# Filter table filled by ScalarE from one PSUM bank and by VectorE from the other, with a new instruction order

## The chip, the cores and the metric

The kernel runs on one core of a Trainium2 chip. It uses five engines: TensorE (PE, matrix products into PSUM), VectorE (DVE), ScalarE (ACT), GpSimd (POOL) and SyncE (SP), which issues the DMAs. The metric is the device time of one execution in microseconds (us), lower being better. Times are medians over several executions; a profile comes from one execution and has a time of its own.

## The reference

Four sequences of 768 steps with 8 heads of width 48 go through a gated linear recurrence; its output, 384 channels wide, goes through a block that multiplies a circular convolution over time (by Fourier transform) with two gates.

```
for t in range(S):                       # S = 768, per batch and head
    cur = outer(u * k[t], v[t])
    y[t] = r[t] @ (state + cur)
    state = w[t][:, None] * state + outer(k[t], v[t])
x = y.transpose(0, 2, 1, 3).reshape(B, S, 384)

proj = x @ w_proj                        # three parts: x1, x2, x3
H = rfft(filter_fft, n=S, axis=0)
x2c = irfft(rfft(x2, n=S, axis=1) * H, n=S, axis=1)
out = (x1 * x2c * x3) @ w_out
```

Inputs and output are float32.

## The kernel before

Each of the 4 sequences is cut into 6 chunks of 128 steps, 24 chunks numbered through. A chunk goes through the function `first`: the running sum of log w by two matrix products (`cs`), its exponential in place in PSUM (`ex`, ScalarE), a product with k and r (`kq`, VectorE, L1344), eight transposes (`tr`), a copy (`qk`), the scores within the chunk (`sc`), their triangular mask (`mt` on VectorE or ScalarE, `mc` on GpSimd where ScalarE made the copy), the state (`ki`, `kv`, `su`), the output (`yi`, `ys`, `y`, `xn`) and its transpose (`yt`, `xT`). Chunks are loaded alone or in pairs by `group`, four loads a chunk (w, k, r, v: `lw`, `lk`, `lr`, `lv`), which also makes the diagonal term (`rk`, `ru`, `rh`, `cc`, `vc`: products of tensors in SBUF).

When a sequence's chunks are done, `second` runs the block: projections `p` and `q` with their gate products (`cp`, `cq`, `gq`), the middle part `xw`, sums and differences of its two halves (`sd`), the forward transform `f` (three blocks of frequencies; copied by `cf` to the tile X), the product with the filter table (`u0`, `u1` into U, their sum into P; that sum's steps are also called `p`, as p0.0 or p3.1, on VectorE, where the projections p0.0.0 are TensorE's), the inverse transform `E` with the sums of even and odd parts (`cE`, `aE`, `dE`), the gate (`yE`), the output projection `o` with its copy `co` and store `so`. The last sequence (3) does this in smaller pieces, so that its stages overlap.

The filter table is made once, by `spectrum`, in the middle of the first second half: `fsd0` and `fsd1` (VectorE) take sum and difference of the two halves of the loaded filter; `h0`, `h1`, `h2` (TensorE) transform them, each into two PSUM banks, one with the cosine part and one with the sine part; and the copies scale both parts into the tile hh, twice each, one sign changed. In the kernel before, `hc` (ScalarE) reads both banks for one half of hh and `hg` (VectorE) reads both banks for the other half. All later `u` read hh.

Nothing schedules this at run time. Every engine runs its instructions in the order in which they stand, and waits by semaphores. The order is a table (`ORDER`, about a thousand lines): each line names a step, the engine that does it (P, A, D, G, S; M and N one instruction over both score banks on VectorE or ScalarE, V an addition on VectorE, C a GpSimd cut over both, "-" not needed), the PSUM bank where it takes one, and sometimes another step after which a GpSimd instruction is made to start (a tie, given to the framework as a dependency with the reason "port"). Lines `warm n` are products of a zero tile without use, placed where TensorE has nothing else. Loads stand in the table too, in the order in which SP issues them.

Of the kernel before, what the change touches and what calls it, by code (L numbers as in the profile page):

```python
# [21 lines left out]
L = 128  # L22
# [15 lines left out]
ADD, DVE2, ACT2, POOL2, FOLD, FULL, BLOCK = "V", "M", "N", "C", "Q", "F", "B"  # L38
# [257 lines left out]
rk4 G
xT4 A
xw0.0 P 0
ex6 A
cq0.2.0 D  # L300
cxw0.0 A
gq0.2.0 -
cs7 P 6
kq6 D
xw0.2 P 2
ex7 A
ph6 A
kq7 D
cxw0.2 A
p0.2.1 P 0  # L310
cp0.2.1 A
ru4 D
xw0.4 P 4
tr6 P 2
tr7 P 0
ph7 A
p0.0.1 P 6
cxw0.4 A
vb4 A
sd0.0.0 D  # L320
sd0.1.0 D
kv6 P 4
qk7 A
su6 D
rh4 D
cc4 D
qk6 A
cp0.0.1 A
q0.2.1 P 5
sc7 P 3  # L330
sc6 P 1
mt6.0 M
mt7.1 -
mt6.1 -
mc7.1 -
mc6.0 -
vc4 G rh4
ki7 P 0
cq0.2.1 D
gq0.2.1 -  # L340
kv7 P
q0.0.1 P 6
cq0.0.1 D
su7 D
f0.2 P 1
mt7.0 N
ln5 A
mc7.0 C
fsd0 D
fsd1 D  # L350
lw14 S
yi6 P 3
in A
cf0.2 A
gq0.0.1 -
mc6.1 -
y6 P
lw15 S
xn6 A
yi7 P 5  # L360
ys7 P
y7 P
xn7 A
cs8 P 0
ex8 A
cs9 P 2
yt7 P 5
lr14 S
lk15 S
lr15 S  # L370
lk14 S
xT7 A
ex9 A
kq8 D
f0.1 P 6
cf0.1 A
lv13 S
lv12 S
kq9 D
h1 P 4  # L380
ph8 A
hg1 D
f0.0 P 6
hc1 A
ph9 A
cf0.0 A
ln6 A
rk5 G fsd1
ru5 D
rh5 G ru5  # L390
h2 P 2
lw17 S
vb5 G ru5
lv17 S
lw16 S
hc2 A
h0 P 4
hg2 D
hc0 A
hg0 D  # L400
yt6 P 2
tr8 P 6
u00.0 D
tr9 P 7
ki8 P 0
kv8 P
xT6 A
qk8 A
sc8 P 5
xw1.0 P 3  # L410
qk9 A
su8 D
lv15 S
mt8.0 N
u10.0 D
ki9 P 2
p0.0 D
sc9 P 0
kv9 P
cxw1.0 A  # L420
mt8.1 -
lk16 S
mc8.1 -
mt9.1 -
lv14 S
lr17 S
lr16 S
lk17 S
mt9.0 N
cs11 P 6  # L430
cs10 P 4
ex10 A
su9 D
kq10 D
ex11 A
warm 5 3
E0.2 P 0
gq0.0.0 -
cc5 D
cwout A  # L440
ph10 A
cE0.2 A
E0.0 P 2
kq11 D
aE0.2.0 D
E0.1 P 4
cE0.0 A
ph11 A
tr11 P 6
aE0.0.1 D  # L450
aE0.0.0 D
mc8.0 C p0.0
vb6 A
aE0.2.1 D
cE0.1 A
mc9.0 C p0.0
vc5 G
tr10 P 7
qk11 A
aE0.1.1 D  # L460
aE0.1.0 D
yi8 P 2
ys8 P
ki10 P 0
qk10 A
y8 P
xn8 A
kv10 P
sc11 P 6
su10 D  # L470
yt8 P 4
yi9 - 0
dE0.2.1 -
sc10 P 2
mt11.0 M
ln7 A
mt11.1 -
mt10.1 -
mc9.1 -
xT8 A  # L480
ys9 P
y9 P
xn9 V
mt10.0 N
cs12 P 4
# [3 lines left out]
rk6 G  # L489
ru6 G  # L490
rh6 D
cc6 D
p1.0.0 P 0
mc10.0 C rh6
vc6 G rh6
kq12 D
ph12 A
lv16 S
lw18 S
lw19 S  # L500
lr19 S
kq13 D
cp1.0.0 A
q1.0.0 P 2
ph13 A
lk19 S
lk18 S
lr18 S
yi11 - 6
yi10 - 0  # L510
tr12 P 4
yt9 P 5
cq1.0.0 D
qk12 A
mc11.1 -
dE0.1.1 -
mc11.0 -
dE0.2.0 -
dE0.1.0 -
dE0.0.0 -  # L520
mc10.1 -
xT9 A
ys10 P
ys11 P
y10 P
y11 P
rk7 G
xn11 V
tr13 P 4
xn10 V  # L530
rk8 G
qk13 A
p1.2.0 P 5
yt11 P 2
xw1.2 P 6
ln8 A
cp1.2.0 A
xT11 A
lw21 S
lv18 S  # L540
lv19 S
lk20 S
yt10 P 4
dE0.0.1 -
yE0.2 D
yE0.0 D
yE0.1 D
sc13 P 0
ru7 D
xT10 A  # L550
gq1.0.0 -
mt13.1 -
cxw1.2 A
cs15 P 2
mt13.0 M
ex15 A
xw1.4 P 4
cs14 P 6
kq15 D
cxw1.4 A  # L560
ex14 A
o0.2 P 0
ph15 A
kq14 D
sd1.1.0 D
rh7 D
p1.0.1 P 4
q1.0.1 P 2
co0.2 A
tr14 P 0  # L570
ph14 A
cp1.0.1 A
cc7 D
cq1.0.1 D
ru8 D
vb7 A
f1.2 P 4
qk14 A
sc14 P 0
sc12 P 6  # L580
mt14.1 -
cf1.2 A
kv12 P 2
mt14.0 N
# [1320 lines left out]
```

## Time and profile before

| quantity | us |
|---|---|
| time, median of 3 runs | 161.98 |
| lowest and highest run | 160.59, 162.64 |
| time of the profiled execution | 161.71 |
| its span, first to last instruction | 159.8 |
| TensorE busy in the span (with the products of the zero tile) | 143.2 |
| VectorE busy | 132.9 |
| ScalarE busy | 128.9 |
| GpSimd busy | 77.6 |

The span begins with the first instruction and ends with the last, after the last store has landed; 1.9 us of the profiled execution lie around it. The busy time of an engine is a sum over stages of different kinds. In the page's 40 slices of 4 us each, the DMA engines are busy to nine or ten tenths up to about 112 us:

```profile
PE   7999868989999568999699999999999999949980
DVE  6446957936898499999997999999999999999920
PEclk9999999999999999999999999999999999995997
DMA  4999899999998999798997999999600340000175
```

Each digit is the share of its slice in tenths. VectorE's digits are low in the first third, where it waits for loads, and full from slice 15 (60 us) to slice 38. The clock granted to TensorE is full but for slice 36 (144 to 148 us) and the end.

### The profile page before, as it was taken

What the parts mean: (1) busy time and instruction counts of PE and PEld (TensorE: products, weight loads), DVE (VectorE), ACT (ScalarE), POOL (GpSimd) and SP (SyncE); (2) the same over time, 40 slices, a digit from 0 to 9 for tenths busy, and PEclk for the clock granted to TensorE, in tenths of its full rate; (3) what the DMA queues carried; (4) which work ended last, traced back from release to release, by engine and by line L of the source; (5) the groups of instructions that cost most, each with busy time, mean ns of one, the idle gap of its engine ahead of it and who ended that gap; (6) DMA issues with size and microseconds to landing.
All of it is one profiled execution on the core that took longest, in us unless ns stands there. A gap on an engine that the chain in (4) does not pass through costs nothing.

```text
span 159.8 us, 4305 instructions
## 1 busy us (share of the span) xinstructions
PE 143.2 (90%) x1675; PEld 91.1 (57%) x1675; DVE 132.9 (83%) x236; ACT 128.9 (81%) x228; POOL 77.6 (49%) x86
## 2 busy tenths in 40 slices
PE   7999868989999568999699999999999999949980
PEld 2356446556666254767467676767667567524540
DVE  6446957936898499999997999999999999999920
ACT  5999967889997779997979899999999676631680
POOL 7842975951261701988506556276166604832000
PEclk9999999999999999999999999999999999995997
DMA  4999899999998999798997999999600340000175
GB/s 88 218 208 218 170 213 258 232 256 187 257 254 171 205 256 181 140 215 168 215 212 156 213 181 193 199 247 275 172 4 0 118 174 7 0 0 4 73 299 218
DMA packets 104117, 27.40 MB, mean 171 GB/s; under 512 B 100129, under 2 KB 102690, under 8 KB 104098
## 3 DMA queue, kind: packets, MB, share of 16 engines
q1 hardware_dynamic: 104098, 27.14, 75.1%
q8 instruction: 13, 0.21, 0.5%
q14 instruction: 6, 0.05, 0.1%
HBM read 22.41 MB, written 4.72 MB: 170 GB/s over the span
## 4 chain that ended last, share of the span: by engine, by line
PE 39%; SPq 20%; DVE 18%; DMA 8%; ACT 6%; issue 4%; POOL 1%; ACTq 1%; DVEq 0%; POOLq 0%
SPq L1301 18%; PE banks L1630 7%; PE banks L1806 7%; DMA kr<-in_r_dram 5%; PE banks L1734 5%; DVE U L1193 4%; PE banks L1356 3%; PE banks L1518 3%; DMA kr<-in_k_dram 3%; DVE hh L1599 2%; PE banks L1670 2%; PE banks L1376 2%; DVE mt L1397 2%; ACT x L1197 2%; DVE kq L1344 2%
## 5 line engine op out<-in xcount | busy, mean ns | idle before, releaser
L1193 POOL TENSOR_TENSOR rk<-kr 128x768 bf16<-128x768 f32 (+1 forms) x13 | 22.4, 1721 | 20.4 <-DMA kr<-in_r_dram 9.8
L1344 DVE TENSOR_TENSOR kq<-banks,kr 128x768 bf16<-128x768 f32 x24 | 22.5, 951 | 7.8 <-ACT banks L1341 4.8
L1630 PE MATMUL banks<-xT,wproj 128*128 128x384 bf16 x144 | 28.8, 339 | 0.0
L1193 POOL TENSOR_TENSOR vc<-vb,cc 128x768 bf16<-128x768 bf16 (+1 forms) x13 | 17.8, 1374 | 14.8 <-DVE rk L1193 6.4
L1197 ACT ACTIVATE x<-banks 128x768 bf16<-128x768 f32 (+1 forms) x29 | 19.8, 701 | 1.9 <-PE banks L1630 0.8
L1397 DVE TENSOR_TENSOR mt<-banks,mask_excl 128x1024 bf16<-128x1024 f32 (+1 forms) x17 | 18.5, 1091 | 1.3 <-PE banks L1376 1.2
L1341 ACT ACTIVATE banks<-banks 128x768 f32<-128x768 f32 x24 | 19.0, 806 | 0.6 <-ACT banks L1341 0.4
L1630 PEld LDWEIGHTS <-wproj 128*128 128x128 bf16 x144 | 13.5, 100 | 8.3 <-issue 1.3
L1402 POOL TENSOR_SCALAR_AFFINE_SELECT mt<-mt 128x1024 bf16<-128x1024 bf16 (+1 forms) x11 | 10.1, 925 | 15.2 <-ACT banks L1341 7.7
L1231 PE MATMUL banks<-wt 128*128 128x512 bf16 (+1 forms) x50 | 14.5, 435 | 1.1 <-DVE scl L1255 1.1
L1240 ACT ACTIVATE qk<-banks 128x512 f32<-128x512 f32 x24 | 13.9, 603 | 0.9 <-PE banks L1356 0.6
L1356 PE MATMUL banks<-ident,kq 128*128 128x128 bf16 x192 | 14.0, 219 | 0.5 <-DVE kq L1344 0.3
L1806 PE MATMUL banks<-wout,y 128*128 128x384 bf16 x72 | 13.0, 326 | 1.4 <-DVE mt L1397 1.3
L1518 PE MATMUL banks<-sd,F 128*128 128x384 bf16 (+1 forms) x96 | 13.6, 327 | 0.0
L1670 PE MATMUL banks<-wproj,xT 128*128 128x384 bf16 x72 | 13.5, 326 | 0.0
L1197 ACT ACTIVATE o<-banks 128x768 f32<-128x768 f32 (+1 forms) x13 | 9.8, 762 | 3.9 <-PE banks L1806 3.9
L1356 PEld LDWEIGHTS <-kq 128*128 128x128 bf16 x192 | 11.5, 97 | 2.3 <-DVE kq L1344 1.0
L1518 PEld LDWEIGHTS <-F 128*128 128x128 bf16 (+1 forms) x120 | 8.7, 103 | 7.2 <-issue 3.0
L1193 DVE TENSOR_TENSOR U<-X,hh 128x2304 bf16<-128x2304 bf16 (+1 forms) x12 | 12.7, 1074 | 0.0
L1734 PE MATMUL banks<-mi,P 128*128 128x384 bf16 (+1 forms) x62 | 10.4, 306 | 2.4 <-DVE P L1707 2.1
L1656 DVE TENSOR_TENSOR g<-banks,x 128x768 bf16<-128x768 f32 (+1 forms) x14 | 10.4, 752 | 1.7 <-PE banks L1630 1.4
L1197 ACT ACTIVATE X<-banks 128x768 bf16<-128x768 f32 x12 | 9.7, 811 | 2.4 <-PE banks L1518 1.2
(111 smaller groups left out, 311.4 us busy)
## 6 DMA issues: line engine op xcount, KB each, us to landing
kr<-in_r_dram SPq DMA_DIRECT2D x24, 192.0 KB, 4.2
w<-in_w_dram SPq DMA_DIRECT2D x24, 192.0 KB, 3.8
kr<-in_k_dram SPq DMA_DIRECT2D x24, 192.0 KB, 4.3
v<-in_v_dram SPq DMA_DIRECT2D x24, 192.0 KB, 4.1
out_dram<-o SPq DMA_DIRECT2D x11, 384.0 KB, 2.3
y<-in_moe_w_proj_dram SPq DMA_DIRECT2D x2, 576.0 KB, 5.1
U<-in_moe_filter_fft_dram SPq DMA_DIRECT2D x1, 1152.0 KB, 7.5
sd<-in_moe_w_proj_dram SPq DMA_DIRECT2D x1, 576.0 KB, 6.5
```

The lines of the kernel that those rows point to most:

```text
L1193: return eng(e).tensor_mul(o, a, b)
L1197: return nc.scalar.activation(out=o, in_=a, func=AF.Copy)
L1301: op(f"l{name}{i}", [SP], lambda e, bk, t=t, x=x, q=q, rw=rw: nc.sync.dma_start(out=t[:, q], in_=x[b, :, rw, :].rearrange("h t d -> t h d" ...
L1341: op(f"ex{i}", [ACT], lambda e, bk: nc.scalar.activation(out=two(bk, f"cs{i}")[:, :, 0:C], in_=two(bk, f"cs{i}")[:, :, 0:C], func=AF.Exp), ...
L1344: op(f"kq{i}", [DVE], lambda e, bk: nc.vector.tensor_mul(kq[f][:, :, :, 0:D], two(bk, f"cs{i}")[:, :, 0:C].rearrange("p a (h d) -> p a h d ...
L1356: nc.tensor.transpose(p[:, HP * m + j, :], kq[f][:, m, 2 * j:2 * j + 2, :], ident)
L1397: return copy(ACT, o, x) if e in (ACT, ACT2) else nc.vector.tensor_mul(o, x, _mid(mask_excl, z - HP * a))
L1518: nc.tensor.matmul(p[rows], F[:, ti, c0 + rows.start:c0 + rows.stop], x[q][:, ti, :], start=(ti == 0), stop=(ti == NT - 1),)
L1630: nc.tensor.matmul(p, wproj[:, cb, col0:col0 + L], xT[bx][:, NT * hf:NT * hf + NT, cb, :], start=(cb == 0), stop=(cb == CB - 1),)
L1670: nc.tensor.matmul(view(bk)[:, z], xT[bx][:, c0 + z, cb, :], wproj[:, cb, C:2 * C], start=(cb == 0), stop=(cb == CB - 1),)
L1734: nc.tensor.matmul(o, P[:, q, m, cs], x, start=start, stop=stop)
L1806: nc.tensor.matmul(view(bk)[:, z], yt_[:, z, :], wout[:, cb, :], start=(cb == 0), stop=(cb == CB - 1),)
```

## The change

Two things are changed. The filter table's copies are divided by bank: `hc` (ScalarE) now reads the cosine bank alone and writes it to both its places in hh with one instruction (a broadcast input, an output of two pieces 9*C apart), also for block 0, where it was two instructions. `hg` (VectorE) reads the sine bank alone and writes its two places; in block 0 a third instruction then overwrites one row, which `hc0` has written before, so `hg0` is declared to come after `hc0`.

```diff
         def hcopy(n):
             def fn(e, bk):
-                p = two(bk, f"h{n}")[:, :, 0:C]
-                if n:
-                    nc.scalar.activation(out=hh[:, 0, :, n, :], in_=p, func=AF.Copy, scale=2.0 / S)
-                    return
-                nc.scalar.activation(out=hh[:, 0, 0, 0, :], in_=p[:, 0], func=AF.Copy, scale=scl0)
-                nc.scalar.activation(out=hh[:, 1, 0, 0, :], in_=p[:, 1], func=AF.Copy, scale=neg0)
+                o = hh[:, 0, 0, n, :]
+                o = dataclasses.replace(o, ap=[o.ap[0], [9 * C, 2], [1, C]])
+                nc.scalar.activation(
+                    out=o, in_=_mid(two(bk, f"h{n}")[:, 0, 0:C], 2), func=AF.Copy, scale=2.0 / S if n else scl0)
             return fn
 
         def gcopy(n):
             def fn(e, bk):
-                p = two(bk, f"h{n}")[:, :, 0:C]
+                p = two(bk, f"h{n}")[:, 1, 0:C]
...
                 if n:
-                    put(hh[:, 1, 1, n, :], p[:, 0], 2.0 / S)
-                    put(hh[:, 1, 0, n, :], p[:, 1], -2.0 / S)
+                    put(hh[:, 0, 1, n, :], p, 2.0 / S)
+                    put(hh[:, 1, 0, n, :], p, -2.0 / S)
                     return
-                put(hh[:, 1, 1, 0, :], p[:, 0], scl0)
-                put(hh[0:1, 1, 1, 0, :], p[0:1, 1], 1.0 / S)
-                put(hh[:, 0, 1, 0, :], p[:, 1], neg0, -1.0)
+                put(hh[:, 0, 1, 0, :], p, neg0, -1.0)
+                put(hh[:, 1, 0, 0, :], p, neg0)
+                put(hh[0:1, 1, 1, 0, :], p[0:1], 1.0 / S)
             return fn
...
-            op(f"hg{n}", [DVE], gcopy(n), r=["smalls"], w=[f"H.{n}"], uses=[f"h{n}"])
+            op(f"hg{n}", [DVE], gcopy(n), r=["smalls"] + ([] if n else ["Hc.0"]), w=[f"H.{n}"], uses=[f"h{n}"])
```

And the whole table is replaced by another: 1000 lines for 1003, with the same steps. Some sixty steps are given to another engine, the ties go from 40 to 43, the uses of the zero tile from 95 units to 83, and a variant of the masked scores that no line of the table used is taken out (with the half mask that it needed, two GpSimd copies of 64 by 64). Two lines of the table's difference:

```diff
-E0.2 P 0
+E0.0 P 4
```

What the new order does at three places. First VectorE in the filter stage, from the sum and difference of the filter (a reading of U, with a wait for a DMA) on; P is their output, kq the product of chunks 8 and 9, hh the table, S a chunk's state. Before:

```order
L1581 TENSOR_TENSOR P_116<-U_117 128x1152 [waits DMAHW6_49]
L1581 TENSOR_TENSOR P_116<-U_117 128x1152
L1344 TENSOR_TENSOR kq0_88<-banks_150,kr1_65 128x16x48 [waits DMAHW7_49,DMAHW1_49,Activation_49]
L1344 TENSOR_TENSOR kq1_89<-banks_150,kr1_65 128x16x48 [waits DMAHW0_49,DMAHW2_49,PE_49,Activation_49]
L1599 TENSOR_SCALAR hh_132<-banks_150 128x384 [waits PE_49] x2
L1193 TENSOR_TENSOR rk2_77<-rk2_77,u_b_149 128x768 [waits Pool_49]
L1599 TENSOR_SCALAR hh_132<-banks_150 128x384 [waits Activation_49]
L1599 TENSOR_SCALAR hh_132<-banks_150 128x384 [waits PE_49]
L1599 TENSOR_SCALAR hh_132<-banks_150,scl0_144 128x384 [waits Activation_49]
L1599 TENSOR_SCALAR hh_132<-banks_150 1x384 [waits DVE_49,Activation_49]
```

With the change:

```order
L1553 TENSOR_TENSOR P_116<-U_117 128x1152 [waits DMAHW5_49]
L1553 TENSOR_TENSOR P_116<-U_117 128x1152
L1413 TENSOR_TENSOR S0_103<-banks_149,phi3_95 128x192 [waits PE_49]
L1338 TENSOR_TENSOR kq1_89<-banks_149,kr1_65 128x16x48 [waits DMAHW7_49,DMAHW1_49,Activation_49]
L1569 TENSOR_SCALAR hh_132<-banks_149 128x384 [waits PE_49]
L1569 TENSOR_SCALAR hh_132<-banks_149 128x384
L1338 TENSOR_TENSOR kq0_88<-banks_149,kr1_65 128x16x48 [waits DMAHW2_49,DMAHW0_49,Activation_49]
L1569 TENSOR_SCALAR hh_132<-banks_149,neg0_144 128x384 [waits PE_49]
L1569 TENSOR_SCALAR hh_132<-banks_149,neg0_144 128x384
L1569 TENSOR_SCALAR hh_132<-banks_149 1x384 [waits Activation_49]
L1569 TENSOR_SCALAR hh_132<-banks_149 128x384 [waits PE_49]
L1569 TENSOR_SCALAR hh_132<-banks_149 128x384
```

The waits of the table's VectorE copies for ScalarE (Activation) have become waits for TensorE, but for the one row of block 0; the product rk (`ru5`) has left VectorE here for GpSimd, and the two kq stand between the copies in the other order.

Next ScalarE in the same stage, where phi is a small exponential, X the forward transform's result, lg the logarithm of w. Before:

```order
L1197 ACTIVATE X_115<-banks_150 128x2x384 [waits PE_49]
L1348 ACTIVATE phi0_92<-banks_150 128x4 [waits DVE_49]
L1588 ACTIVATE hh_132<-banks_150 128x2x384 [waits DVE_49]
L1348 ACTIVATE phi1_93<-banks_150 128x4 [waits Activation_49]
L1197 ACTIVATE X_115<-banks_150 128x2x384 [waits PE_49]
L1307 ACTIVATE lg0_72<-w0_61 128x16x48 [waits DMAHW4_49,DMAHW3_49]
L1588 ACTIVATE hh_132<-banks_150 128x2x384 [waits PE_49]
L1590 ACTIVATE hh_132<-banks_150,scl0_144 128x384 [waits PE_49]
L1591 ACTIVATE hh_132<-banks_150,neg0_145 128x384 [waits PE_49]
```

With the change:

```order
L1335 ACTIVATE banks_149<-banks_149 128x2x384 [waits PE_49]
L1560 ACTIVATE hh_132<-banks_149 128x2x384 [waits PE_49]
L1342 ACTIVATE phi1_93<-banks_149 128x4 [waits DVE_49]
L1560 ACTIVATE hh_132<-banks_149,scl0_143 128x2x384 [waits PE_49]
L1193 ACTIVATE vb1_82<-v1_69 128x768 [waits DMAHW4_49,DMAHW3_49]
L1193 ACTIVATE X_115<-banks_149 128x2x384 [waits PE_49]
L1342 ACTIVATE phi0_92<-banks_149 128x4 [waits DVE_49]
L1560 ACTIVATE hh_132<-banks_149 128x2x384 [waits PE_49]
```

The three steps of hh now wait for TensorE alone, the first no longer stands behind a VectorE copy, block 0 takes one instruction, and the conversion of v for chunks 8 and 9 (`vb5`, waiting for two loads) has come in between from GpSimd.

Last, the sequence 3 tail on VectorE, from the even and odd sums of sequence 2 (y from banks and ev) through the three products with hh of sequence 3 (U, then P). Before:

```order
L1769 TENSOR_TENSOR y_121<-ev0_118,banks_150 128x2x192 [waits PE_49,Activation_49]
L1764 TENSOR_TENSOR y_121<-banks_150,ev0_118 128x2x192
L1193 TENSOR_TENSOR U_117<-X_115,hh_132 128x2x384 [waits Activation_49]
L1777 TENSOR_TENSOR y_121<-y_121 128x384 [waits DVE_49]
L1193 TENSOR_TENSOR U_117<-X_115,hh_132 128x2x384
L1193 TENSOR_TENSOR U_117<-X_115,hh_132 128x2x384 [waits Activation_49]
L1777 TENSOR_TENSOR y_121<-y_121 128x384
L1193 TENSOR_TENSOR U_117<-X_115,hh_132 128x2x384
L1707 TENSOR_TENSOR P_116<-U_117 128x2x384 [waits DVE_49]
L1707 TENSOR_TENSOR P_116<-U_117 128x2x384
```

With the change:

```order
L1739 TENSOR_TENSOR y_121<-ev0_118,banks_149 128x2x192 [waits PE_49,Activation_49]
L1734 TENSOR_TENSOR y_121<-banks_149,ev0_118 128x2x192
L1747 TENSOR_TENSOR y_121<-y_121 128x384 [waits DVE_49]
L1189 TENSOR_TENSOR U_117<-X_115,hh_132 128x2x384 [waits Activation_49]
L1189 TENSOR_TENSOR U_117<-X_115,hh_132 128x2x384
L1677 TENSOR_TENSOR P_116<-U_117 128x2x384 [waits DVE_49]
L1189 TENSOR_TENSOR U_117<-X_115,hh_132 128x2x384 [waits Activation_49]
L1189 TENSOR_TENSOR U_117<-X_115,hh_132 128x2x384
L1677 TENSOR_TENSOR P_116<-U_117 128x2x384 [waits DVE_49]
L1189 TENSOR_TENSOR U_117<-X_115,hh_132 128x2x384 [waits Activation_49]
L1189 TENSOR_TENSOR U_117<-X_115,hh_132 128x2x384
L1677 TENSOR_TENSOR P_116<-U_117 128x2x384 [waits DVE_49]
```

The three pairs of U now stand each directly before their P; the steps of y between them (`dE`) have gone ahead of them or behind, and frequency block 2 comes first where it came last. On GpSimd, the rows beside this were three `sd`, two `dE`, a gate product of 768 (`yE2.1`) and `gq3.2.0`; now they are `dE1.1.1`, two `sd`, one `dE`, `gq3.2.0` and a gate product of 384 (`yE3.1.0`).

Among the steps given to another engine behind chunk 12's product `kq12`, VectorE loses eleven instructions (`mt17.1`, `cq2.0.0`, `mt18.1`, `mt19.0`, `xn18`, `dE1.0.0`, `dE1.0.1`, `sd3.0.0`, `dE2.2.1`, `cq3.0.1`, `yE3.1.0`) and gains twelve (`mt17.0`, `xn16`, `mt18.0`, `rh11`, `mt21.1`, `gq2.0.0`, `sd3.0.1`, `sd3.1.2`, `dE2.1.0`, `dE2.1.1`, `yE2.1`, `gq3.0.1`), and `mt16.0` grows from one bank to two. TensorE has one product pair `yi` less. In the loads, the filter's is issued one load earlier, before w of chunk 9; r of chunk 8 comes fifth behind it instead of first; and the last loads of k and r come ahead of the first stores.

1633 lines of the change are left out of this document (803 added, 830 removed).

## The prediction

> **What bounds the kernel now.** The page's busy time of each engine comes first, then the span of 159.8 us cut into stages.
>
> ```profile
> PE 143.2 (90%) x1675; PEld 91.1 (57%) x1675; DVE 132.9 (83%) x236; ACT 128.9 (81%) x228; POOL 77.6 (49%) x86
> ```
>
> The stage table gives, for each stretch, its length, the busy time of PE, PE's weight loads, DVE, ACT and POOL (instructions in brackets), the granted clock, the DMA engines' share and GB/s.
>
> ```profile
> 47.00:63.20 16.20, 12.60 (x155) 7.70 (x151) 12.95 (x18) 12.82 (x23) 3.66 (x4) 1.00 0.97 202
> 63.20:100.00 36.80, 35.37 (x480) 24.59 (x481) 35.29 (x56) 33.27 (x63) 22.84 (x16) 1.00 0.95 188
> 100.00:131.00 31.00, 30.86 (x445) 21.42 (x443) 30.49 (x53) 27.72 (x53) 14.85 (x13) 1.00 0.56 142
> 131.00:143.20 12.20, 10.10 (x74) 6.05 (x72) 12.08 (x21) 7.34 (x13) 6.68 (x6) 1.00 0.08 30
> 143.20:155.30 12.10, 12.04 (x63) 6.60 (x63) 9.24 (x21) 5.99 (x10) 0.91 (x1) 0.86 0.28 106
> ```
>
> From 63.2 to 131 us TensorE is busy for 66.2 of 67.8 us and VectorE for 65.8: two engines at their limit at once. From 131 to 143 VectorE alone is full and TensorE waits. Only before 63.2 do both have room: in the filter stage (47 to 63.2) each is idle for over 3 us, while the DMA engines are at 0.97. So no rearrangement in the middle can win much; time can be won by starting the full stretch earlier, by taking waste out of VectorE's work in it, or in the tail.
>
> **The filter stage.** The timeline of that stage, VectorE first, then one row of ScalarE and two of TensorE (start, length, operation; in brackets the idle time before it and what ended it):
>
> ```profile
> 47.10 2.62 DVE L1581 TENSOR_TENSOR P<-U 128x1152 bf16<-128x1152 f32 x2
> 49.64 0.95 DVE L1344 TENSOR_TENSOR kq<-banks,kr 128x768 bf16<-128x768 f32 x1
> 51.15 0.96 DVE L1344 TENSOR_TENSOR kq<-banks,kr 128x768 bf16<-128x768 f32 x1 [0.57 <-DMA kr<-in_k_dram]
> 52.03 1.01 DVE L1599 TENSOR_SCALAR hh<-banks 128x384 bf16<-128x384 f32 x2
> 53.13 0.56 DVE L1193 TENSOR_TENSOR rk<-rk,u_b 128x768 bf16<-128x768 bf16 x1
> 56.11 1.02 DVE L1599 TENSOR_SCALAR hh<-banks 128x384 bf16<-128x384 f32 x2 [2.43 <-ACT hh L1588]
> 57.05 0.61 DVE L1599 TENSOR_SCALAR hh<-banks,scl 128x384 bf16<-128x384 f32 x1
> 58.87 1.36 DVE L1193 TENSOR_TENSOR U<-X,hh 128x2304 bf16<-128x2304 bf16 x1
> 60.15 0.35 DVE L1432 TENSOR_TENSOR S<-banks,phi 128x192 bf16<-128x192 f32 x1
> 60.41 1.35 DVE L1193 TENSOR_TENSOR U<-X,hh 128x2304 bf16<-128x2304 bf16 x1
> 61.80 1.36 DVE L1707 TENSOR_TENSOR P<-U 128x2304 bf16<-128x2304 bf16 x1
> 53.08 0.81 ACT L1588 ACTIVATE hh<-banks 128x768 bf16<-128x768 f32 x1 [2.22 <-DVE hh L1599]
> 54.00 1.62 PE L1518 MATMUL banks<-P,F 128*128 128x384 bf16 x9 [1.19 <-ACT phi L1348]
> 63.21 1.47 PE L1734 MATMUL banks<-mi,P 128*128 128x384 bf16 x8 [0.35 <-ACT banks L1341]
> ```
>
> The two engines take turns on the table: ScalarE's first copy waits 2.22 us until VectorE's is done, VectorE's next waits 2.43 us for ScalarE's, and TensorE's h2 waits behind them. From the start of `fsd0` (47.10) to the end of P (63.16) VectorE takes 16.06 us.
>
> Divided by bank, `hc` and `hg` of one block run beside each other. Counted from start to start in these rows, the changed chain on VectorE is: fsd 2.54, the state step 0.26, a kq 0.88, `hg1` 1.10, the other kq 0.88, `hg0` 1.82, `hg2` 0.94, a state step 0.26, then U, U and P from 58.87 to 63.16, that is 4.29 without the state step already counted, less 0.26: 4.03. The sum is 12.7 us, so 3.35 less; `ru5`, part of the 16.06, is GpSimd's here. The filter's load is issued one load earlier, worth about 0.8 at most. The upper bound for the earlier start is 4.2 us. ScalarE's table work is three copies of 0.81, all beside VectorE's. What is late next is a load: `vb5` waits on ScalarE for v of chunks 8 and 9, with X, the exponential phi and `hc2` queued behind it, and U waits for `hc2`. In the stream they take the place of w of chunks 10 and 11, which landed near 52 (the second was issued at about 48, the landing time of a load stands below), so `hc2` ends near 55 (a conversion, X, phi and a table copy behind it, some 2.7 us), about when VectorE comes to U: no cost as I count it, up to 1 us if a load is late. `hg0`'s new wait for `hc0` hides behind its own first two copies (1.1 us for one ScalarE copy of 0.81).
>
> **How much of it reaches chunk 12.** An earlier start asks for earlier data. The DMA queue's issues, the time to landing of such a load, VectorE's products of chunks 12 and 13, and the DMA engines' share in the stretch (DMA 0.87 of 10 us):
>
> ```profile
> 47.38 2.64 SPq L1301 DMA_DIRECT2D w<-in_w_dram  x2
> 65.13 1.48 SPq L1301 DMA_DIRECT2D kr<-in_r_dram  x2
> kr<-in_r_dram SPq DMA_DIRECT2D x24, 192.0 KB, 4.2
> 71.27 1.81 DVE L1344 TENSOR_TENSOR kq<-banks,kr 128x768 bf16<-128x768 f32 x2
> 60.00:70.00 10.00, 1.00 0.87 173
> ```
>
> r of chunk 12, issued at 65.13, is there at 69.3; its product starts at 71.27. The changed table has this chunk's last load at the same place of the stream. If the stream keeps its pace, at most 2.0 us of the gain pass this point, and `kq12` starts at 69.3. If the 0.13 that the DMA engines were idle there is used, 1.3 more can pass. Bounds 0 and 4.2; I take 2.0, by the row that is nearest.
>
> **VectorE's work from `kq12` to the end.** Before, from 71.27 to the last VectorE instruction:
>
> ```profile
> 151.92 1.16 DVE L1193 TENSOR_TENSOR y<-y,g 128x384 bf16<-128x384 bf16 x4
> L1397 DVE TENSOR_TENSOR mt<-banks,mask_excl 128x1024 bf16<-128x1024 f32 x13 | 15.8, 1216 | 1.2 <-PE banks L1376 1.2
> L1397 DVE TENSOR_TENSOR mt<-banks,mask_excl 128x512 bf16<-128x512 f32 x4 | 2.6, 682 | 0.1
> L1656 DVE TENSOR_TENSOR g<-banks,x 128x768 bf16<-128x768 f32 x7 | 6.7, 954 | 1.6 <-PE banks L1630 1.4
> ```
>
> It ends at 153.08, after 81.8 us. The steps that change engines nearly cancel: lost are three masks at 0.68, two gate products at 0.95 and six small ones of 0.35 to 0.55; gained are one mask at 1.22, two at 0.68, one that doubles (0.53) and nine of 0.35 to 0.55. That makes 6.3 off and 7.1 on: 0.8 us more work.
>
> What can shrink is waiting inside VectorE's own instructions:
>
> ```profile
> 76.14 2.18 POOL L1193 TENSOR_TENSOR rk<-kr 128x768 bf16<-128x768 f32 x1 [0.94 <-DMA kr<-in_k_dram]
> 76.58 2.17 DVE L1193 TENSOR_TENSOR rk<-rk,u_b 128x768 bf16<-128x768 bf16 x1
> L1193 DVE TENSOR_TENSOR rk<-rk,u_b x11: 350/558/2165, 15.4 to 123.9; 128x768 bf16<-128x768 bf16 x9, 128x384 bf16<-128x384 bf16 x2
> 137.00 2.16 POOL L1777 TENSOR_TENSOR y<-y 128x384 bf16<-128x384 bf16 x2 [0.34 <-DVE y L1777]
> 138.31 1.07 DVE L1777 TENSOR_TENSOR y<-y 128x384 bf16<-128x384 bf16 x1
> 139.52 1.82 POOL L1193 TENSOR_TENSOR y<-y,g 128x768 bf16<-128x768 bf16 x1 [0.36 <-DVE y L1777]
> 139.77 1.99 DVE L1193 TENSOR_TENSOR U<-X,hh 128x768 bf16<-128x768 bf16 x1
> 141.68 0.35 DVE L1777 TENSOR_TENSOR y<-y 128x384 bf16<-128x384 bf16 x1
> L1193 DVE TENSOR_TENSOR U<-X,hh x4: 545/552/1990, 137.8 to 141.9; 128x768 bf16<-128x768 bf16 x4
> ```
>
> Three VectorE products of two SBUF tensors take 2.17, 1.07 and 1.99 us where their like take 0.56, 0.35 and 0.55 (minimum, median and longest stand in the x11 and x4 rows), and each ends just after a GpSimd instruction that overlaps it. Together they lose 1.6 + 0.7 + 1.4 = 3.8 us. The changed table puts the two tail products on VectorE and smaller pieces on GpSimd, each tied behind a step that sums from PSUM follow; the first collision hangs on when loads of chunks 14 and 15 land, and nothing in the table forbids it. Bounds 0 and 3.8 saved; I take half, 1.9, since the tail's 2.1 look safe and the early one may come back with others.
>
> The Trainium skill, SBUF — State Buffer, section "Who interferes with whom", says that VectorE with two SBUF inputs and a GpSimd instruction that reads SBUF exclude each other for a whole instruction, and that whichever issues first decides who blocks. The three rows agree with it. By that rule a tie alone does not protect the next VectorE product, the tail's 2.1 would be saved, the 1.6 not, and the sum would be 0.2 us shorter (158.5).
>
> **The sum.** Start of `kq12` 2.0 earlier, 0.8 more work, 1.9 less waiting: 3.1 us off VectorE's end. Behind it stand the last products, copies and stores, which stay as they are. The zero tile's products fall by 12 units, all in stretches where TensorE waits: nothing. TensorE does the same products as before, less one pair of 128x192, and stays covered by VectorE. So 161.71 of the profiled execution becomes 158.6; the median of the runs shown lies 0.27 above it, and stays within that, so I give **158.7 us** for the time, against 161.98.
>
> **The tail** gets no term of its own, since VectorE carries it:
>
> ```profile
> 143.15 0.86 PE L1734 MATMUL banks<-mi,P 128*128 128x384 bf16 x4 [2.10 <-DVE P L1707]
> 143.81 3.08 PE L1630 MATMUL banks<-xT,wproj 128*128 128x384 bf16 x9
> ```
>
> TensorE waits 2.10 us for P, and the nine products behind it take 3.08 us at a clock that the stage table gives as 0.86 in the mean; at half clock 1.5 of it would be lost. With P in three separate pairs the wait may go; between 0 and 3.6 us of TensorE time, covered by VectorE up to its end.
>
> **The rivals.** *The loads hold everything.* With the DMA engines at 0.95 to 0.97 up to 100 us, an earlier start may only move waits to later loads: then `kq12`'s 2.0 shrink to about 0.5 and VectorE idles instead. With half the port term: 0.5 + 1.9 - 0.8, time 160.4. For it speaks the share, against it, that the share falls to 0.56 from 100 us on, so that the stream is ahead there. *Both gains in full:* 4.2 + 3.8 - 0.8 = 7.2 is the limit, 5 a likely size, time 157; it needs the loads to speed up. *The edit does nothing:* if the two copies still take turns, or the broadcast copy of ScalarE takes longer than 0.81, the stage keeps its 16 us and the work term and collisions decide: 161 to 162.
>
> *The slower side: the tail's POOL steps.* `sd3.0.0` is now tied on GpSimd behind `gq2.0.1`, and f3.1 and f3.0 wait for it. If VectorE comes to it over 1.3 us later than TensorE's queue allows, TensorE stands still before some 8 us of products. In the rows above 2.10 us of idleness preceded the half clock. With the clock halved for two stretches as long as that one (1.5 us each) and 2 us of waiting, less 1 of the saved start: 4 more, 166. The Trainium skill, TensorE: Matmul & The Clock Gate, section "What's actually happening", gives an idle window of about 3.4 us before the clock halves; here 2.1 us were enough, and by that rule the rival would need a longer wait.
>
> **Chances.** The forecast's case 0.45; loads hold 0.20; both in full 0.20; the edit does nothing 0.08; tail slower 0.07. A measurement of this kernel tells about 2% from no change, here 3.2 us: under 158.74 is faster. The forecast lies on that edge: half of its case (0.22 or 0.23) and the full case make faster 0.43; the other half, the holding loads and the idle edit make within 2% 0.50; the tail makes slower 0.07. The range, 155.8 to 162.2, leaves out the limit of both gains below and the tail rival above.
>
> **What would show it.** Right: in the changed profile ScalarE's and VectorE's copies into hh overlap, P of sequence 0 ends 12 to 13 us after the first fsd, the first E starts at 59 to 61 instead of 63.2; `kq` of chunk 12 at 69 to 70, ended by a wait for in_r or in_k; no U or y product of 128x768 above 1 us after 130; no TensorE wait for P over 1 us. Wrong: an E that starts at 62 or later, new VectorE waits for loads between 70 and 110 that sum to over 2 us, or new collisions with GpSimd of over 3 us.

## The result and the profile after

The changed kernel takes 156.94 us (median of 4, 156.10 to 157.53) against 161.72 of the kernel before on the same chip (median of 4, 160.59 to 162.64): ratio 0.970, 95% interval 0.962 to 0.978, so faster by 3%. The forecast was 158.7. The profiled execution took 156.10, its span is 154.0.

The page's busy time and slices of the changed kernel:

```profile
PE 141.9 (92%) x1666; PEld 89.3 (58%) x1666; DVE 127.6 (83%) x237; ACT 127.9 (83%) x225; POOL 76.9 (50%) x85
...
PE   4999887789999999999999999999999999999880
...
DVE  6306795985799999999999699999989899999930
...
PEclk9999999999999999999999999999999999999999
DMA  4999989997999899899996999989970000700185
```

VectorE does one instruction more than before and is busy 5.3 us less; the slice of low clock is gone. By stages (columns as in the prediction's table):

```profile
46.80:60.00 13.20, 12.72 (x159) 7.83 (x157) 12.70 (x18) 13.20 (x24) 4.69 (x4) 1.00 1.00 211
60.00:100.00 40.00, 39.31 (x520) 26.56 (x520) 37.65 (x60) 35.98 (x69) 23.39 (x17) 1.00 0.98 193
100.00:131.00 31.00, 30.77 (x427) 21.10 (x426) 29.52 (x54) 25.85 (x49) 15.48 (x13) 1.00 0.47 110
131.00:143.20 12.20, 11.68 (x81) 6.78 (x80) 11.99 (x28) 7.86 (x13) 2.07 (x3) 1.00 0.25 98
```

In the 13.2 us of the filter stage TensorE, VectorE and ScalarE have 0.5 us of room or less. In the last window TensorE is busy for 11.7 of 12.2 us, where it was 10.1; counted from the start of sequence 2's P, which comes 3.5 us earlier now (128.02 against 131.49), it is 12.2 against 10.1. The filter stage on VectorE (first block), then the three copies of ScalarE:

```profile
46.93 2.67 DVE L1553 TENSOR_TENSOR P<-U 128x1152 bf16<-128x1152 f32 x2
...
51.22 1.01 DVE L1569 TENSOR_SCALAR hh<-banks 128x384 bf16<-128x384 f32 x2
52.15 0.95 DVE L1338 TENSOR_TENSOR kq<-banks,kr 128x768 bf16<-128x768 f32 x1
53.01 1.14 DVE L1569 TENSOR_SCALAR hh<-banks,neg 128x384 bf16<-128x384 f32 x2
54.06 1.46 DVE L1569 TENSOR_SCALAR hh<-banks 1x384 bf16<-1x384 f32 x3
...
58.55 1.36 DVE L1677 TENSOR_TENSOR P<-U 128x2304 bf16<-128x2304 bf16 x1
```

```profile
51.15 0.84 ACT L1560 ACTIVATE hh<-banks 128x768 bf16<-128x768 f32 x1
...
51.89 0.95 ACT L1560 ACTIVATE hh<-banks,scl 128x768 bf16<-128x768 f32 x1
...
54.28 0.81 ACT L1560 ACTIVATE hh<-banks 128x768 bf16<-128x768 f32 x1
```

ScalarE's first copy (51.15 to 51.99) lies beside VectorE's two (51.22 to 52.23); neither engine waits for the other, and P ends at 59.91, 12.98 us after the first fsd.

To see where the 5.8 us went, the program is cut at five instructions, whose times stand in each kernel's timeline: the start of `fsd0`, the end of sequence 0's P, the start of chunk 12's `kq`, the start of sequence 2's P, and the issue of the last store. All experiments are in the table.

| kernel | to fsd0 | fsd0 to P | P to kq12 | kq12 to P of seq. 2 | P to last store | sum | median us |
|---|---|---|---|---|---|---|---|
| before | 47.10 | 16.05 | 8.11 | 60.22 | 24.77 | 156.26 | 161.72 |
| changed | 46.93 | 12.98 | 8.86 | 59.25 | 22.46 | 150.48 | 156.94 |
| edit_alone | 49.09 | 13.05 | 8.10 | 58.77 | 23.70 | 152.72 | 157.95 |
| order_alone | 46.72 | 15.57 | 8.99 | 59.14 | 22.45 | 152.88 | 158.69 |
| new_to_chunk10 | 46.78 | 14.22 | 12.22 | 58.76 | 23.70 | 155.68 | 162.23 |
| new_from_chunk10 | 48.31 | 15.91 | 9.36 | 61.23 | 22.46 | 157.27 | 162.74 |
| early_tie | 46.68 | 16.37 | 8.11 | 58.75 | 23.70 | 153.61 | 160.15 |
| tail_no_gpsimd | 48.22 | 15.82 | 8.11 | 60.21 | 23.32 | 155.67 | 161.78 |
| old_tail | 47.12 | 13.42 | 9.21 | 59.35 | 25.60 | 154.70 | 159.78 |
| new_tail | 46.74 | 16.19 | 8.12 | 60.22 | 22.10 | 153.36 | 159.65 |
| fill_wait | 46.98 | 16.11 | 8.11 | 60.23 | 23.71 | 155.15 | 161.75 |
| no_ties | 46.79 | 14.55 | 8.69 | 60.40 | 24.26 | 154.69 | 162.14 |
| old_order_new_ends | 49.20 | 13.05 | 8.11 | 58.74 | 22.09 | 151.19 | 155.69 |
| pairs_first | 47.74 | 16.65 | 8.11 | 60.28 | 22.82 | 155.59 | 160.98 |

Row against row, the change gained 0.17, 3.07, -0.75, 0.97 and 2.31: 5.8 in all. The stretches come from one execution each, the medians from 4 to 12 (before: 161.5 to 162.0 beside the experiments). Ratios below leave disturbed executions out, so they need not be the quotient of the medians.

### The profile page after: what moved, and what is told of

The parts are those of the page before. It is cut to its first block, busy times and chain, and to the rows that moved or that the text cites. A ratio compares the mean times of both kernels' runs of the same rounds, so it can differ in the third digit from the quotient of the medians.

```text
span 154.0 us, 4271 instructions
## 1 busy us (share of the span) xinstructions
PE 141.9 (92%) x1666; PEld 89.3 (58%) x1666; DVE 127.6 (83%) x237; ACT 127.9 (83%) x225; POOL 76.9 (50%) x85
## 4 chain that ended last, share of the span: by engine, by line
PE 47%; DVE 28%; ACT 11%; issue 5%; POOL 2%; DMA 1%; POOLq 1%; ACTq 0%; SPq 0%; DVEq 0%
PE banks L1600 11%; PE banks L1640 6%; DVE U L1189 5%; PE banks L1350 4%; PE banks L1225 4%; DVE kq L1338 4%; PE banks L1362 3%; ACT banks L1335 3%; PE banks L1441 3%; PE banks L1490 3%; DVE mt L1378 2%; PE banks L1704 2%; DVE P L1677 2%; PE banks L1461 2%; PE banks L1776 2%
## 5 line engine op out<-in xcount | busy, mean ns | idle before, releaser
L1600 PE MATMUL banks<-xT,wproj 128*128 128x384 bf16 x144 | 27.5, 326 | 0.1
L1600 PEld LDWEIGHTS <-wproj 128*128 128x128 bf16 x144 | 12.8, 97 | 7.4 <-issue 0.5
L1225 PE MATMUL banks<-wt 128*128 128x512 bf16 (+1 forms) x43 | 13.6, 471 | 1.1 <-DVE wt L1256 1.1
L1453 DVE TENSOR_TENSOR xn<-banks,vc 128x384 bf16<-128x384 f32 x17 | 9.2, 552 | 3.6 <-PE banks L1441 3.6
L1383 POOL TENSOR_SCALAR_AFFINE_SELECT mt<-mt 128x1024 bf16<-128x1024 bf16 (+1 forms) x10 | 9.5, 954 | 5.0 <-DVE P L1677 4.0
L1189 DVE TENSOR_TENSOR U<-X,hh 128x2304 bf16<-128x2304 bf16 (+1 forms) x12 | 11.2, 966 | 0.0
```

Of the source, the lines that this page charges most:

```text
L1189: return eng(e).tensor_mul(o, a, b)
L1225: nc.tensor.matmul(banks[:, int(at), 0:256 * z], wt[:, 0:L], _mid(wt, z), start=True, stop=True)
L1600: nc.tensor.matmul(p, wproj[:, cb, col0:col0 + L], xT[bx][:, NT * hf:NT * hf + NT, cb, :], start=(cb == 0), stop=(cb == CB - 1),)
```

## The experiments

In a kernel made of both orders, the table of one runs up to a named step and is followed by the lines of the other that are not done yet.

**edit_alone**: the edit without the order.

```diff
 (kernel before, its ORDER)
-hcopy, gcopy, hg as before
+hcopy, gcopy, hg as in the change
```

> The kernel before with its own order; only the copies of the filter table are divided by bank. Theory A (the two engines' turns on the table cost the filter stage about 3 us, and most of it passes chunk 12): ScalarE's first copy no longer waits 2.2 us for VectorE, nor VectorE's next 2.4 us for ScalarE; the stage from the first fsd to the end of P falls from 16.1 to 13 to 14.5 us, kq of chunk 12 starts 1.5 to 2.5 earlier, and the time falls by 1.3 to 2.5 us (159.2 to 160.4). Rival B (the gain is the new order's, the edit alone only moves the wait): stage 15.5 or more, time within 0.7 us of before.

Measured: 157.95, ratio 0.973 (0.966 to 0.980). The stage falls from 16.05 to 13.05, nearly as far as in the changed kernel (12.98). ScalarE's copies in this kernel (before, the first stood behind 2.22 us of waiting):

```profile
52.69 0.81 ACT L1588 ACTIVATE hh<-banks 128x768 bf16<-128x768 f32 x1
55.55 0.79 ACT L1588 ACTIVATE hh<-banks 128x768 bf16<-128x768 f32 x1
56.24 0.89 ACT L1588 ACTIVATE hh<-banks,scl 128x768 bf16<-128x768 f32 x1
```

The waits are gone, and B falls. The edit owns the 3.0 us. kq12 starts only 1.0 earlier, since fsd0 started 2.0 later, and the time is under A's range. The other parts of its 3.54 are not shown to be the edit's: 2.0 lost before fsd0, 1.45 won between kq12 and sequence 2 (no collision at `ru7`), 1.07 won in the tail (no half clock); both gains come back below. For the collision, VectorE's `ru7` and the GpSimd product that met it before (rk8):

```profile
75.55 0.56 DVE L1193 TENSOR_TENSOR rk<-rk,u_b 128x768 bf16<-128x768 bf16 x1
77.11 1.82 POOL L1193 TENSOR_TENSOR rk<-kr 128x768 bf16<-128x768 f32 x1 [2.93 <-DMA kr<-in_k_dram]
```

Here VectorE is through with `ru7` before the load that releases rk8 has landed; before, rk8 started 0.44 us ahead of it. Both kernels with the new copies, the old order behind the filter stage and no tie are free of the collision (this one and new_to_chunk10), and all five such kernels with the old copies have it, at `ru7` or at a gate product beside it, so the earlier stage may be its cause; no run separates that from chance.

**order_alone**: the order without the edit.

```diff
 (changed kernel, its ORDER)
-hcopy, gcopy, hg as in the change
+hcopy, gcopy, hg as before
```

> The changed kernel with its new order, but the copies of the filter table as before, so that each bank pair is read by VectorE and ScalarE in turn. Theory A: the stage takes 15 to 16.5 us instead of 13.0, kq of chunk 12 starts 2 to 3 later than in the changed kernel, time 158.5 to 160 (1.5 to 3 over the changed kernel). Rival B (the order carries the gain and has slack for the turns): time within 0.7 us of the changed kernel, 156.3 to 157.6.

Measured: 158.69, ratio 0.983 (0.977 to 0.988) to before, 1.75 over the changed kernel. The turns are back, on ScalarE:

```profile
53.29 0.81 ACT L1560 ACTIVATE hh<-banks 128x768 bf16<-128x768 f32 x1 [2.26 <-DVE hh L1571]
54.05 0.58 ACT L1562 ACTIVATE hh<-banks,scl 128x384 bf16<-128x384 f32 x1
54.51 0.59 ACT L1563 ACTIVATE hh<-banks,neg 128x384 bf16<-128x384 f32 x1
57.42 0.81 ACT L1560 ACTIVATE hh<-banks 128x768 bf16<-128x768 f32 x1 [0.82 <-DVE hh L1571]
```

The stage takes 2.6 us more than with the edit, the last store is 2.4 later, and all stretches behind stay within 0.15. Theory A holds; the order alone is worth 3.3 us by the medians, behind the filter stage. The two gains overlap: edit alone 4.0, order alone 3.3, together 4.8, since neither profile shows the collision at `ru7` or the half clock in the tail.

**new_to_chunk10 and new_from_chunk10**: the two orders joined behind the filter stage.

```diff
 (new_to_chunk10)
 ORDER of the change up to cs10
+ORDER before, from there
 (new_from_chunk10)
 ORDER before up to cs11, with the old copies
+ORDER of the change, from there
```

> The changed kernel up to the cumulative sums of chunk 10 (its head, its filter stage, its copies), and from there the old order. Theory A (two gains that add: the earlier start about 2.5, the work behind it about 2.5 of collisions less the added work): the start's part stays, the collisions of the old order come back (a GpSimd product beside a VectorE product of two SBUF tensors at three places, 3 to 4 us of excess), time 158.7 to 160.0. Rival B (the old order waits for loads and gives the start back): kq of chunk 12 as early as in the changed kernel, but the time within 0.8 us of before, 161 to 162.

> The kernel before up to the cumulative sums of chunk 10 (its head, its filter stage with its old copies), and from there the new order. Theory A: first E at 62 to 63.5 as before, hardly any collisions behind it (under 1 us of excess in VectorE's products), time 158.5 to 160.0; this run and new_to_chunk10 together save about what the whole change saves (4.8). Rival B (the new order needs the earlier start, and waits otherwise): time 161 or more.

Measured: 162.23 (1.004, 1.000 to 1.008) and 162.74 (1.003, 0.999 to 1.008). The first misses both theories (kq12 starts at 73.22, later than before); the second lies in rival B's range of times, but B's waiting is not all that it shows. The joint itself costs time in both. In the first TensorE stands at the joint and then runs the sums E slowly (timeline):

```profile
62.24 0.32 PE L1330 MATMUL banks<-lg,mask_neg 128*128 128x384 bf16 x1 [2.27 <-DVE S L1414]
...
63.99 4.25 PE L1705 MATMUL banks<-mi,P 128*128 128x384 bf16 x17
```

These 17 products take 4.25 us, and over most of that, up to 66.6 us, the clock granted to TensorE is 0.50. P to kq12 takes 12.22 instead of 8.1 to 8.9. So this run doesn't show whether the old order can use the start; edit_alone does. In the second, collisions come back, though its order from there is the new one (VectorE, and the form of its costliest product; then GpSimd):

```profile
77.57 2.18 DVE L1192 TENSOR_TENSOR y<-y,g 128x768 bf16<-128x768 bf16 x1
```

```profile
L1680 DVE TENSOR_TENSOR sd<-x x10: 351/746/2411, 42.1 to 139.3; 128x1152 bf16<-128x1152 bf16 x6, 128x384 bf16<-128x384 bf16 x4
```

```profile
77.51 1.82 POOL L1192 TENSOR_TENSOR rk<-kr 128x768 bf16<-128x768 f32 x1 [0.78 <-DMA kr<-in_r_dram]
```

GpSimd, released by a load, starts 0.06 us before VectorE's product, which then takes 2.18 instead of 0.55. Freedom from collisions belongs to the order together with its times. The Trainium skill, SBUF — State Buffer, "Who interferes with whom", says that the port pair which VectorE and GpSimd share is an exclusive lock, and that the order of issue decides who blocks; these two rows agree.

**early_tie**: one GpSimd step tied, in the kernel before.

```diff
-rk8 G
...
 ru7 D
+rk8 G ru7
```

> The kernel before with one GpSimd step, rk of chunks 14 and 15 (rk8), made to start only after VectorE's ru7; nothing else. Theory A (the product ru7 lost 1.6 us to that GpSimd step, and VectorE is the path there): ru7 takes 0.55, kq of chunk 16 starts 1.3 to 1.8 earlier relative to kq of chunk 12, and the time falls by 1.2 to 1.8 us (160.1 to 160.7). Rival C (the loss was a chance of one execution, since loads decide when rk8 starts, or rk8's later end is waited for instead): time within 0.6 us of before.

Measured: 160.15 against 161.53, ratio 0.998 (0.994 to 1.003). In the profile the price is what theory A said:

```profile
76.47 0.55 DVE L1193 TENSOR_TENSOR rk<-rk,u_b 128x768 bf16<-128x768 bf16 x1
```

kq12 to sequence 2 falls from 60.22 to 58.75, by 1.47. In four other old-order kernels with the old copies and no tie (tail_no_gpsimd, new_tail, fill_wait, pairs_first) that stretch is 60.2 to 60.3, though `ru7` is free in them: rk8 meets the gate product beside it instead. The medians lie 1.4 us apart, but the interval does not reach a gain of 0.9%, so the runs leave open how often an execution pays it.

**tail_no_gpsimd and pairs_first**: the port in the tail.

```diff
-dE2.1.0 G dE2.2.0
-dE2.1.1 G dE2.2.0
-yE2.1 G dE2.0.1
+dE2.1.0 D
+dE2.1.1 D
+yE2.1 D
 (pairs_first also: on VectorE u and p of sequence 3 before
  dE2.0.1, dE2.2.1, cq3.2.1; yE2.1 right behind dE2.1.1)
```

> The kernel before with three steps of its tail given from GpSimd to VectorE, as the change does (dE2.1.0, dE2.1.1, yE2.1), at their old places in the table. Theory A (GpSimd beside VectorE cost 2.1 us there): VectorE gains 1.25 of work and loses 2.1 of waiting, TensorE's wait for P falls from 2.1 to 0.1 to 1.3 us, and the products behind it are likelier to run at full clock; from p2.0 to the last store 22.5 to 24.0 us against 24.8, time 160.0 to 161.2. Rival D (what the new tail wins is the order of the TensorE products and of the three pairs of U and P, not the port): 23.5 to 24.8 us, time within 0.5 us of before.

> As tail_no_gpsimd (three steps of the old tail given to VectorE), and on VectorE the three pairs of U and P of sequence 3 before the steps dE2.0.1, dE2.2.1 and cq3.2.1, and yE2.1 directly behind the last dE2.1 instead of after E3's first sums. In tail_no_gpsimd the P of sequence 3 came 2.2 us earlier against p2.0, and TensorE then waited 2.19 us for yE2.1. Theory A (the port's 2.1 us are real and were given back to that wait): TensorE's wait before the second output projection falls from 2.19 to under 0.8, from p2.0 to the last store 22.3 to 23.0 us against 23.3 and 24.8, time 159.5 to 161. Rival D (only the new tail's TensorE order with frequency block 2 first wins the rest): 23.2 us or more, time as before.

Measured: 161.78 (1.005, 1.001 to 1.010), over A's range of times and within D's, though with a tail of 23.32 as A had it; and 160.98 (0.990, 0.983 to 0.997). The first shows a gain that turns into another wait (TensorE):

```profile
141.86 0.82 PE L1734 MATMUL banks<-mi,P 128*128 128x384 bf16 x4
142.52 1.63 PE L1630 MATMUL banks<-xT,wproj 128*128 128x384 bf16 x9
...
147.98 0.83 PE L1806 MATMUL banks<-wout,y 128*128 128x384 bf16 x4 [2.19 <-DVE y L1193]
```

The wait for P (2.10 before) is gone, since P comes 2.2 us earlier against sequence 2's P; then TensorE waits 2.19 for the gate product that VectorE now does late. With it done early (pairs_first):

```profile
146.88 0.97 PE L1806 MATMUL banks<-wout,y 128*128 128x384 bf16 x4 [0.63 <-DVE y L1193]
```

the tail takes 22.82, 0.9 under the 23.7 of the old tail at full clock; wait, tail and time lie in theory A's ranges.

**old_tail and new_tail**: the tail as a block.

```diff
 (old_tail)
 ORDER of the change up to f3.2
+ORDER before, from there
 (new_tail)
 ORDER before up to f3.0, with the old copies
+ORDER of the change, from there
```

> The changed kernel, but from the forward transform of sequence 3 on the old order. In the runs so far the old tail takes 23.7 us from p2.0 to the last store with TensorE at full clock and 24.8 with nine products at half clock, the new one 22.5, whatever stands ahead. Theory A (the parts of the program add up): 1.2 to 2.3 us over the changed kernel, 158.2 to 159.3, with the two slow VectorE products (1.07 and 1.99) back. Rival D as it concerns the sum (only the whole order is fast): 160 or more.

> The kernel before, its copies and its order, but from the forward transform of sequence 3 on the new order. Theory A: the tail takes 22.4 to 23.0 us from p2.0 on, without products of TensorE at half clock, time 159.4 to 160.8 (1.2 to 2.3 under before). Rival: the tail's gain needs the rest of the new order, time within 0.5 us of before.

Measured: 159.78 (0.992, 0.987 to 0.997), 2.8 over the changed kernel, and 159.65 (0.994, 0.989 to 0.998). new_tail's time is in theory A's range; its tail of 22.10 is 0.3 shorter than A said. old_tail is 0.5 slower than its range, at the joint: TensorE's forward transform waits 1.67 us there for a sum on VectorE, so 25.60 is no fair price of the old tail.

**fill_wait**: TensorE's order alone.

```diff
 cp3.0.1 A
+q3.2.0 P 7
+q3.0.1 P 0
 E3.0 P 4
 E3.1 P 2
...
-q3.2.0 P 7
-q3.0.1 P 0
```

> The kernel before with one move on TensorE: the products q3.2.0 and q3.0.1 of the last projection go ahead of E3.0 and E3.1 instead of behind them, as in the new order. Nothing on VectorE or GpSimd. Theory D (the new tail wins by what stands where TensorE waited 2.1 us for P): the wait for P falls to 0.3 to 0.8 us, the nine products run at full clock, and from p2.0 to the last store 22.2 to 23.3 us against 23.7 (24.8 with half clock), time 0.5 to 2 us under before. Theory A as it concerns the tail (VectorE carries it, TensorE is covered): 23.5 to 23.8 us, and a gain only in those executions that would have had the half clock.

Measured: 161.75, ratio 1.000 (0.996 to 1.003). The wait for P is cut, and nothing comes of it:

```profile
143.10 1.15 PE L1734 MATMUL banks<-mi,P 128*128 128x384 bf16 x6 [0.55 <-DVE P L1707]
145.56 1.15 PE L1734 MATMUL banks<-mi,P 128*128 128x384 bf16 x6 [1.31 <-DVE P L1707]
```

2.10 us became 0.55, and 1.31 for the next P: 23.71 in all. VectorE carries the tail; D falls as a cause by itself.

**no_ties**: the changed kernel without its ties.

```diff
-rk0 G ru1
+rk0 G
 (and so for all 43)
```

> The changed kernel without its 43 ties: each GpSimd step starts when its inputs are there, and its place on GpSimd stays. Theory E (without ties, GpSimd's products of SBUF tensors fall beside VectorE's): the excess over the shortest of their kind in VectorE's instructions rises from 1.8 to 4 to 8 us, and the time by 1.5 to 5 us (158.5 to 162). Rival F (the ties are spare; the order alone keeps them apart): within 0.7 us of the changed kernel.

Measured: 162.14, ratio 0.998 (0.994 to 1.002) to before: the whole gain is gone, 5.2 us over the changed kernel and just over theory E's range. The excess of VectorE's instructions over the shortest of their form sums to 7.7 us, against 1.8 with ties. The sums P, of the changed kernel and of this one (shortest, median, longest):

```profile
L1677 DVE TENSOR_TENSOR P<-U x6: 557/958/1358, 58.6 to 139.6; 128x2304 bf16<-128x2304 bf16 x3, 128x768 bf16<-128x768 bf16 x3
```

```profile
L1677 DVE TENSOR_TENSOR P<-U x6: 557/1254/2129, 59.2 to 143.3; 128x2304 bf16<-128x2304 bf16 x3, 128x768 bf16<-128x768 bf16 x3
```

Of the 4.2 us between the two last stores, 1.6 lie in the filter stage, 1.2 in the middle and 1.8 in the tail, less 0.3 in the other two stretches. Rival F falls.

**old_order_new_ends**: the parts that paid, together.

```diff
 (kernel before)
+hcopy, gcopy, hg as in the change
+rk8 G ru7
 ORDER before up to f3.0
+ORDER of the change, from there
```

> The old order with three of the parts tried so far: the copies divided by bank, rk8 tied behind ru7, and the new order from the forward transform of sequence 3 on. If the stretches add up as they stood in the other runs (start to fsd0 46.7 to 49.1 in the old order, fsd0 to kq of chunk 12 21.2, from there to p2.0 58.8, from there to the start of the last store 22.1 to 22.5), the last store starts at 148.8 to 151.6 against 150.5 in the changed kernel: time 154.4 to 157.2, as fast as the changed kernel or up to 1.5% faster. Rival G (a gain in one stretch is lost in the next, since loads and GpSimd meet at other moments): 158 or more.

Measured: 155.69 (155.21 to 157.08), ratio 0.966 (0.962 to 0.971). The four stretches behind fsd0 are 13.05, 8.11, 58.74 and 22.09, each as in the kernel it was taken from. Its median is 1.25 under the changed kernel's, on another chip and with intervals that overlap: at least as fast, not shown faster.

## Why the prediction was right in sign and 2 us short

**The filter stage** was forecast at 12.7 and took 12.98; the first E starts at 59.97. Right, and edit_alone shows that the copies are the cause.

**"How much of it reaches chunk 12"** gave 2.0, since r of chunk 12 was to land at 69.3. The size was near (kq12 starts 2.5 earlier), but by luck: this step failed. The load was issued at 62.41, 2.7 us earlier than before, and kq12 is not ended by a load at all (VectorE):

```profile
66.26 1.82 DVE L1378 TENSOR_TENSOR mt<-banks,mask_excl 128x512 bf16<-128x512 f32 x2
68.04 0.55 DVE L1314 TENSOR_REDUCE cc<-rk 128x16 f32<-128x384 bf16 x1
68.51 0.35 DVE L1236 COPY xT<-banks 128x384 bf16<-128x384 bf16 x1
68.77 1.81 DVE L1338 TENSOR_TENSOR kq<-banks,kr 128x768 bf16<-128x768 f32 x2
```

No bracket stands in these rows: VectorE comes from its own work. I read a landing time two us ahead of a use as a limit, with no wait in the rows. All of the stage's 3.07 passes; 0.75 is lost to work that the new order puts between P and kq12 (8.86 us against 8.11 in nearly every kernel of the old order). The loads follow their consumers: between 47 and 70 us of the changed kernel SP's queue waits 2.1 us for ScalarE's exponential and 1.1 for its logarithm, so an earlier stage asks earlier.

**VectorE's added work**, 0.8 from kq12 on: with the collision away the old order needs 58.75 to sequence 2's P, the new 59.25, so 0.5 of it shows there.

**The port term**, 1.9 of 3.8, was the mis-sized one. The early collision, called not safe, is gone (1.47 in early_tie); the 2.1 in the tail are gone too, and pairs_first shows 0.9 of them at the end. Excess in VectorE's instructions falls from 6.4 to 1.8 us. What I weighed wrongly is how order and ties work together. The early collision needs no tie to be gone: rk8 has none in the new table either, but `ru7` runs there at 72.29, and the next GpSimd product waits for its load until 77.35. And I asked whether a single collision was forbidden, where 43 ties together are worth 5.2 us (no_ties). The caution had its ground, as new_from_chunk10 shows. There the joint seems to bring the collisions back, and not lateness alone: order_alone, 2.5 us late at kq12, keeps its 59.14.

**The tail**, which got no term, gave 2.31: 1.24 against the old tail at full clock (23.70, three times) and 1.07 from the half clock that fell in the profiled execution of before. The low clock is a small part of the whole gain: of the 92 executions of before beside the experiments, the 21 with a mean granted clock of 0.998 or more have a median of 161.2, against 161.6 for all. VectorE does carry it, as fill_wait shows; but the reorder lets P come earlier: in the tail of the changed kernel TensorE waits at most 0.3 us for a P, and the six U products of sequence 3 take 0.55 us each.

Of the forecast's 1.1 behind kq12, about 0.3 belong to the middle (half of the early collision, 0.8, less 0.5 of work) and 0.8 to the tail. So the missing 2.5 of the profiled times are 0.5 at kq12, 0.7 in the middle (0.97 against 0.3), 1.5 in the tail (2.31 against 0.8), less 0.2 around the span.

**The rivals.** *Loads hold everything* falls: no VectorE wait for a load from 60 to 131 us, and between 60 and 70 us the DMA engines' share rose from 0.87 to 1.01. *The edit does nothing* falls by edit_alone. *The tail's tie of sd3.0.0* falls: its products wait for no GpSimd step there (a weight load of the output projection waits 0.5 us for a gate product on GpSimd). *Both gains in full*, 157, came nearest, though not because the loads sped up by themselves: they were asked for earlier.

## What to carry to other kernels

A landing time shortly ahead of a use is no limit as long as the using engine's row shows no wait; follow the engine's own queue first, then ask for buffers. Price ties and orders as a set, under their own times: one part taken over is often paid back at the joint or to the next wait (2.10 to 2.19 in tail_no_gpsimd). And before a waiting engine gets work to fill its wait, ask who carries the stretch (fill_wait: nothing).

## What the hardware did that I had not expected

**The same wait, two clocks.** TensorE waited 2.10 us for P in before and in edit_alone. Windows of before, then of edit_alone (columns as above; the clock is the third from the end):

```profile
143.00:145.00 2.00, 1.85 (x8) 1.01 (x9) 1.97 (x6) 0.00 (x0) 0.00 (x0) 0.70 0.03 8
145.00:147.00 2.00, 2.00 (x8) 0.91 (x6) 1.85 (x5) 0.49 (x1) 0.00 (x0) 0.50 0.00 0
```

```profile
141.00:143.00 2.00, 2.00 (x15) 1.18 (x12) 1.97 (x5) 0.49 (x1) 0.00 (x0) 1.00 0.05 8
143.00:145.00 2.00, 2.00 (x14) 1.15 (x13) 1.97 (x5) 0.98 (x2) 0.44 (x1) 1.00 0.00 0
```

The nine products behind it took 3.08 us there and 1.63 here; early_tie (2.10) and new_to_chunk10 (2.09) stayed at full clock too. So "2.1 us were enough" in my prediction holds for one execution in four. The Trainium skill, TensorE: Matmul & The Clock Gate, "What's actually happening", has a free-running window of about 3.4 us, so that the place of the wait in it would decide. The traces fit that. Between the first and the last product, the low clock comes in eight stretches in the 14 traces, each 3.41 us long, and the times from one change of the clock to the next are multiples of that (in new_to_chunk10 the low one is 63.26 to 66.67; the full one behind it lasts 92.16, 27 times 3.41). Laid out on that grid, the stretch that held most of the wait, in before, edit_alone, early_tie and new_to_chunk10:

```profile
140.39:143.80 3.41, 1.31 (x9) 0.60 (x7) 3.38 (x6) 0.81 (x1) 0.95 (x1) 1.00 0.00 0
137.04:140.45 3.41, 1.54 (x10) 0.70 (x8) 3.38 (x5) 1.62 (x3) 1.82 (x1) 1.00 0.00 0
139.95:143.36 3.41, 1.79 (x11) 1.09 (x12) 3.38 (x8) 0.45 (x1) 0.00 (x0) 1.00 0.03 5
141.77:145.18 3.41, 1.55 (x10) 0.97 (x11) 3.38 (x8) 0.33 (x2) 0.06 (x1) 1.00 0.00 0
```

In before the wait lies whole in one stretch, in which TensorE is busy for 1.31 us, and the low clock follows at 143.80. In the others its ends lie in two stretches, TensorE is busy for 1.54 us or more in each, and the clock stays. The 2.27 us of new_to_chunk10's joint left 1.15 us busy in its stretch, and there the low clock followed. So a stretch need not be wholly idle for the clock to fall. No run moved a wait on purpose, and busy time is not the whole rule: in the heads of six other kernels the low clock follows stretches with 1.8 to 2.2 us busy.

**The head is uneven in one order and even in the other.** fsd0, which needs the filter's load, starts between 46.68 and 49.20 us in nine kernels of the old head and between 46.72 and 47.12 in five of the new. In the late ones VectorE waits for that load (1.47 us in old_order_new_ends). The low clock in the head is not the cause: it stands in early_tie (46.68) and not in old_order_new_ends (49.20). Why the load is late was not tried.
